# Attention with routed experts on one core: query and key loads moved on the load queue, and the first slots' routing tables counted in another way

## The chip, the cores and the metric

One core of one Trainium2 chip runs the whole program. The metric is device time in microseconds (us) of one execution, lower is better; several executions are timed and their median is given. Beside the timed executions there is one profiled execution, whose trace is quoted here.

The engines are named as the profile names them: PE is TensorE (matmuls and transposes), DVE is VectorE, ACT is ScalarE, POOL is GpSimd, SP is SyncE, which here only issues DMAs. An engine's DMA issues appear under its name with a q (SPq, POOLq).

## The reference: what is computed

Attention over q, k, v of shape (8, 12, 448, 64): each row of q and k is normalised by its root mean square and scaled by a gain, then a softmax over 448 keys, then the product with v. The result, seen as 3584 tokens of 768 columns, goes through a layer of 8 experts, of which each token uses the one with the largest gate logit.

```python
q_n, k_n = rmsnorm(q, g_q), rmsnorm(k, g_k)
attn = softmax(q_n @ k_n.T / sqrt(64))            # per batch and head
x = (attn @ v).transpose(0, 2, 1, 3).reshape(3584, 768)
logits = x @ w_gate + modality_bias[modality_id]  # 8 experts
e_idx = argmax(logits); gate_w = softmax(logits)[e_idx]
out[t] = gate_w[t] * (relu(x[t] @ w1[e]) @ w2[e])   # e = e_idx[t]
```

## The kernel before

**Units and beats.** Attention is cut into 48 units, each of one batch element and two heads. A unit takes seven beats, and beat n of the program is column block j = n mod 7 of unit i = n // 7. The steps of all units are laid out by hand over the beats, from beat -22 to 335; the table `PLAN` and the function `when` (line 1272) say at which beat each step of unit u is issued. Every engine works through its own instructions in the order in which they were issued, and waits on semaphores where it needs another engine's result.

**The steps of a unit.** `load` (line 789) fetches q and k of a unit, or of two units at once, from device memory by a DMA of SP; the buffers `r1` hold six units of each, so the load of unit u overwrites unit u - 6. `sumsq` squares on ACT (tile `xrw` from `r`) and sums on DVE; `rstd` makes the reciprocal root; `norm` multiplies on POOL (`xrw` from `r` and `at_hlw`; it is the last reader of the loaded buffer). `tr` transposes on PE, and ACT and DVE copy the result as a high and a low part into `xw` and `w1w`; 64-partition pieces of these are then moved by DMAs of SP (line 882, `w1w<-xw` and `w2ha<-xw`), eight per unit, four after the key's transpose and four after the query's. `sa` (line 946) multiplies queries by keys for the row maximum, which DVE takes; `mt` (line 957) transposes the seven maxima, and one small DMA of SP (line 962) puts them where `st` needs them. `st` (line 974) are the scores again, transposed and with the maximum inside; ACT takes the exponent; `av` (line 1013) is the product with v; POOL and DVE add the columns for the softmax sums (`csum`).

Relative to unit u (beat 7u is its first `st`), the key's transpose is at beat 7u - 21, the query's at 7u - 18, the first `sa` at 7u - 14, `mt` at 7u - 6, the squares at 7u - 50 (q) and 7u - 49 (k), and the norm at 7u - 26. From unit 10 on, loads come for two units at a time: the key's at beat 7u - 57, the query's at 7u - 54, u even. The first units have beats of their own in `PLAN["first"]`. Before the first beat the queue gets the loads of units 0, 1, then 2 and 3 together, the four gain loads, then 4 and 5 together; 6 and 7 follow together at beat -12, the key's first.

**Small steps in between.** Routing needs many steps on a few elements per partition. They stand in two lists (`fast`, `slow`), and `pump` (line 1191) takes one or two per beat and issues them between the steps of attention; most are DVE instructions (line 53 in the trace, through the wrapper `Deferred`).

**Tables of the first slots.** After the tokens of six of the eight batch elements have been routed, `tables1` (line 1215) makes index tables for the first three slots of the expert layer. A slot is one expert's block of 256 tokens. `blocks` turns the eight counts into whole blocks by a cast, a shift and a cast back, `prefix` adds them up in three rounds of a copy and an add, and `tables` (line 211) makes from this the slot's expert, its first row, its rows of the list and its rows of the weights. For these tables `taken` is None; `tables2` calls the same function for the other slots later, with `taken` given.

**Expert layer.** Fourteen slots follow, each two matrix products in three passes of high and low parts (`ph`, line 565; `py`, line 595), with weights and tokens gathered by DMAs of POOL.

`gate_consts` (line 148), which makes routing constants on POOL, is issued at beat `PLAN["gc"]` = 24. `warm` (line 1221) puts matmuls on nothing into the beats before attention is under way; they feed no result.

Of the kernel before, what the change touches and what calls it, by code (L numbers as in the profile page):

```python
# [66 lines left out]
def kernel(  # L67
# [80 lines left out]
    def gate_consts():  # L148
# [8 lines left out]
        for tf, ti in iotas:  # L157
            GP.tensor_copy(out=tf, in_=ti)
        GP.tensor_scalar(out=ie8, in0=i_e[:, 0:NE], scalar1=float(NE), scalar2=None, op0=ALU.add)
# [15 lines left out]
    i_vt = iota_f("i_vt", [128, 4], [[128, 4]], cm=1)  # L175
    i_tok = cp.tile([CP, B, NCH], I32, name="i_tok")
# [33 lines left out]

    def tables(nm, ns, cnt, nb, taken, e_prev, half_blocks=None):
# [18 lines left out]
        ci = prefix(nb, nm + "_px", nv)  # L230
        dd = tl("dd", [128, nv])
        V.tensor_tensor(out=dd, in0=nb, in1=ci, op=ALU.subtract)
# [24 lines left out]
        def sel(src, n_):  # L257
            r = tl(n_, [128, ns])
            V.tensor_tensor(out=t3, in0=oh, in1=src.unsqueeze(1).to_broadcast(sh), op=ALU.mult)
            V.tensor_reduce(out=r, in_=t3, op=ALU.add, axis=AX.X)  # L260
            return r
# [3 lines left out]
        V.tensor_tensor(out=js, in0=js, in1=isb, op=ALU.add)  # L265
# [4 lines left out]
        V.tensor_scalar(out=eb, in0=es, scalar1=float(NT), scalar2=None, op0=ALU.mult)  # L270
        V.scalar_tensor_tensor(out=js, in0=js, scalar=float(TB), in1=eb, op0=ALU.mult, op1=ALU.add)
        V.tensor_tensor(out=cs, in0=cs, in1=eb, op=ALU.add)
# [8 lines left out]
        V.tensor_scalar(out=eb[:, 0:nn], in0=js[:, 0:nn], scalar1=float(NE * NT - TB), scalar2=0.5,  # L281
# [487 lines left out]
    if True:  # L769
# [365 lines left out]
        def route_pos(b):  # L1135
# [26 lines left out]
            if b == NB1 - 1:  # L1162
                state["runa"] = cp.tile([128, NE], F32, name="runa")
                V.tensor_copy(out=state["runa"], in_=state["run"])
# [50 lines left out]
        def tables1():  # L1215
            nb1 = blocks(state["runa"], "nb1", 0)
# [10 lines left out]
        for u, n in ((0, 1), (1, 1), (2, 2)):  # L1227
            load(u, n)
        load_gains()
        load(4, 2)  # L1230
# [44 lines left out]
        for u in range(NU):  # L1275
# [23 lines left out]
            if u == 6:  # L1299
                put(-12, "load", u, 2, (1, 0))  # L1300
            elif u in (8, 9):
                put(when("ld", u), "load", u)
            elif u > 9 and u % 2 == 0:
                put(when("ld", u) + 1, "load", u, 2, (1,))
                put(when("ld", u) + 4, "load", u, 2, (0,))

        for n in range(P["start"], NJ * NU):
# [86 lines left out]
            if n == P["lz"]:  # L1394
                SY.dma_start(l_d.rearrange("(p r) w -> p (r w)", p=128), zt)
            if n == P["gc"]:
# [222 lines left out]
```

## Time and profile before

| | us |
|---|---|
| Median of 3 timed executions | 1083.87 |
| Lowest and highest of them | 1081.62 and 1086.3 |
| The profiled execution, its own time | 1088.99 |
| Its span, first to last instruction | 1087.2 |
| PE busy in the span | 1047.1 (96%) |
| DVE busy | 782.4 (72%) |
| POOL busy | 704.7 (65%) |
| ACT busy | 696.1 (64%) |
| Mean granted PE clock, of full speed | 0.986 |

Attention lies from the start to about 585 us, the slots of the expert layer from there to 1058 us, and a short end after that. In the trace, a row of the timeline gives the start, the time it lasted, the engine, the line, the operation, the tile written and the tiles read; an "xN" row merges N instructions; brackets give the idle time of that engine before the row and what released it. L52 and L53 are the wrapper's lines, so such rows are told apart by their tiles.

### The profile page before, as it was taken

The page shows a single profiled execution, that of the slowest core. Times are in us where ns is not written, and L with a number is a line of the kernel's source. Part 1 is how long each engine was busy: PE and PEld are TensorE (multiplying, and loading weights), DVE is VectorE, ACT ScalarE, POOL GpSimd, SP SyncE. Part 2 cuts the span into 40 slices and gives each one's busy share as a digit, 9 for nine tenths or more (in the row PEclk, how much of TensorE's full clock was granted, in tenths as well). Part 3 has the DMA queues.
Part 4 walks back from the last instruction along what each step waited for, and adds up shares of the span by engine and source line. Part 5 has one row for each costly group of instructions (what it writes and reads, how often), then busy time and mean ns, then how long its engine had stood idle before and what let it go on. Part 6 is the DMA issues. An engine that isn't in the chain of part 4 may idle for free.

```text
span 1087.2 us, 18988 instructions
## 1 busy us (share of the span) xinstructions
PE 1047.1 (96%) x6536; PEld 808.6 (74%) x6536; DVE 782.4 (72%) x1351; ACT 696.1 (64%) x1293; POOL 704.7 (65%) x728
## 2 busy tenths in 40 slices
PE   8899999989999999999999999999999999999996
PEld 7645555545555555555556999999999999999995
DVE  5676778968779887798878897667655676566740
ACT  6787888868888787786665555555545555455531
POOL 6787777777876878688776566664455544656451
PEclk9899999989999999999999999999999999999998
DMA  7775767757876669673684822533284422244161
GB/s 177 173 179 123 167 161 170 176 122 163 169 163 165 154 168 165 151 166 90 131 263 132 219 61 78 155 119 93 55 289 147 117 85 67 84 117 117 46 219 61
DMA packets 151704, 153.72 MB, mean 141 GB/s; under 512 B 73434, under 2 KB 141486, under 8 KB 151088
## 3 DMA queue, kind: packets, MB, share of 16 engines
q1 hardware_dynamic: 126244, 110.59, 42.7%
q0 software_dynamic: 25328, 41.82, 12.4%
q8 instruction: 54, 0.88, 0.4%
q14 instruction: 50, 0.41, 0.2%
q10 hardware_dynamic: 28, 0.01, 0.0%
HBM read 150.31 MB, written 33.39 MB: 169 GB/s over the span
## 4 chain that ended last, share of the span: by engine, by line
PE 74%; DMA 8%; DVE 6%; issue 5%; POOL 4%; ACT 2%; SPq 0%; POOLq 0%; DVEq 0%; ACTq 0%
PE ph L565 19%; PE py L595 18%; PE av L1013 11%; PE st L974 11%; DMA w1w<-xw 5%; PE sa L946 4%; PE tr L869 3%; PE xt L1070 2%; DVE at_hlw L52 2%; POOL r2w L52 1%; PE sm L1028 1%; POOL xrw L52 1%; PE warm L1223 1%; ACT xw L52 1%; DVE xw L52 1%
## 5 line engine op out<-in xcount | busy, mean ns | idle before, releaser
L565 PE MATMUL ph<-xw,w1w 128*128 128x256 f32 x2016 | 246.6, 283 | 1.4 <-DVE xw L52 0.8
L565 PEld LDWEIGHTS ph<-xw,w1w 128*128 128x128 f32 x2016 | 244.0, 192 | 3.8 <-issue 1.4
L52 DVE TENSOR_REDUCE at_hlw<-sa 128x1 f32<-128x448 f32 x336 | 205.7, 617 | 42.8 <-PE sa L946 24.4
L974 PE MATMUL st<-w1w 128*128 128x448 f32 (+1 forms) x480 | 177.1, 418 | 0.8 <-DMA w1w<-xw 0.6
L946 PE MATMUL sa<-w1w 128*128 128x448 f32 (+1 forms) x288 | 112.2, 390 | 20.0 <-ACT w1w L52 5.8
L52 POOL TENSOR_TENSOR r2w<-r2w 128x448 f32<-128x448 f32 (+1 forms) x72 | 82.1, 1140 | 64.4 <-DVE r2w L52 23.8
L52 ACT ACTIVATE r2w<-st 128x448 f32<-128x448 f32 x168 | 90.7, 543 | 48.5 <-PE st L974 40.6
L974 PEld LDWEIGHTS st<-w1w 128*128 128x128 f32 (+1 forms) x480 | 85.4, 191 | 45.4 <-ACT r2w L52 15.6
L52 POOL DMA_INDIRECT r<-in_moe_w_dram,tb_w x60 | 78.1, 1301 | 57.8 <-DVE w1w L52 42.5
L595 PE MATMUL py<-w2lw,hhw 128*128 128x384 f32 x448 | 113.7, 334 | 0.0
L52 ACT ACTIVATE hhw<-ph 128x512 fp32r<-128x512 f32 x56 | 33.5, 598 | 120.9 <-PE ph L565 102.0
L52 DVE TENSOR_TENSOR w1w<-r,w1w 128x768 fp32r<-128x768 f32 x112 | 103.4, 953 | 8.9 <-ACT w1w L52 7.3
L52 ACT CAST w1w<-xw 64x448 fp32r<-64x448 f32 x188 | 105.5, 561 | 3.4 <-issue 1.4
L52 POOL DMA_INDIRECT r2w<-in_moe_w_dram,tb_vi x48 | 51.0, 1062 | 86.3 <-DVE w2lw L52 73.7
L52 DVE TENSOR_TENSOR w2lw<-r2w,w2ha 128x1536 fp32r<-128x1536 f32 x28 | 49.1, 1757 | 79.2 <-issue 50.3
L52 ACT ACTIVATE at_w2lw<-st 128x448 f32<-128x448 f32 x168 | 90.5, 544 | 22.6 <-PE st L974 17.5
L974 PE MATMUL st<-w1w,w2ha 65*128 65x448 f32 x288 | 101.1, 371 | 1.1 <-DMA w1w<-xw 1.1
L52 POOL TENSOR_TENSOR xrw<-r,at_hlw 112x512 f32<-112x512 f32 x95 | 98.0, 1051 | 5.0 <-PE tr L869 4.5
L52 ACT CAST w1w<-r 128x768 fp32r<-128x768 f32 x112 | 95.0, 901 | 0.0
L946 PEld LDWEIGHTS sa<-w1w 128*128 128x128 f32 (+1 forms) x288 | 55.8, 194 | 35.1 <-issue 10.5
L52 POOL TENSOR_TENSOR r2w<-r2w,at_w2lw 64x448 f32<-64x448 f32 (+1 forms) x48 | 54.7, 1140 | 41.8 <-DVE r2w L52 18.1
L595 PEld LDWEIGHTS py<-w2lw,hhw 128*128 128x128 f32 x448 | 80.9, 188 | 0.0
(313 smaller groups left out, 2208.5 us busy)
## 6 DMA issues: line engine op xcount, KB each, us to landing
w1w<-xw SPq DMA_DIRECT2D x312, 112.0 KB
xg<-xrw SPq DMA_DIRECT2D x14, 768.0 KB
xrw<-xg SPq DMA_DIRECT2D x56, 192.0 KB
r<-in_q_dram SPq DMA_DIRECT2D x22, 448.0 KB
r<-in_k_dram SPq DMA_DIRECT2D x22, 448.0 KB
w2ha<-xw SPq DMA_DIRECT2D x72, 112.0 KB
r2w<-in_v_dram SPq DMA_DIRECT2D x24, 224.0 KB
at_w2lw<-in_v_dram SPq DMA_DIRECT2D x24, 224.0 KB
```

Of the source, the lines that this page charges most:

```text
L52: return fn(*a, **kw)
L565: PE.matmul(ps[:, i], lhsT=lt_, rhs=rt_[:, c], start=n == 0, stop=n == 17)
L595: PE.matmul(ps[n][:, :384], lhsT=lt_[:, j, 128 * t : 128 * t + 128], rhs=rt_[:, 384 * n : 384 * n + 384], start=j == 0 and m == 0, stop=j ...
L869: PE.transpose(sp[:, c], src[:, c], idn[:CP, :CP])
L946: PE.matmul(ps[:, :S], lhsT=t["qq"][r, h, a : a + 128], rhs=t["kk"][h][r], start=True, stop=True)
L974: PE.matmul(ps[:, :S], lhsT=l, rhs=t["qq"][:, h] if first else t["ql"][:, h], start=first and (j != 3 or h == 0), stop=not first and (j != ...
L1013: PE.matmul(t["av"][64 * h : 64 * h + 64, :S], lhsT=vv[r, u % 3, j], rhs=t["p"][r, j], start=c == 0, stop=c == 3)
L1028: PE.matmul(R[g][32 * i : 32 * i + 32, :S], lhsT=sel[:, m], rhs=T[u + i // 2]["cs"][:, i % 2], start=m == 0, stop=False, tile_position=(0, ...
L1070: PE.transpose(ps[:CP, 128 * c : 128 * c + 128], T[u]["xt"][:, c * CP : (c + 1) * CP], idn)
L1223: PE.matmul(wps[:, :128], lhsT=ones, rhs=idn, start=True, stop=True)
```

## The change

Two parts, which share no instruction.

**Loads.** Units 0 to 5 are loaded one by one ahead of the first beat (two loads of 224 KB each, instead of pairs of 448 KB for units 2 and 3, 4 and 5). Units 6 to 9 are loaded one by one at beat 7u - 58 (beat -16 for unit 6, -9 for unit 7; unit 9 keeps its own beat 6). From unit 10 on the pair's query load is at beat 7u - 59, where it was at 7u - 54, and the key load stays at 7u - 57, so the query now comes first.

**Tables of the first slots.** Whole blocks are counted by one comparison of the eight counts with ten thresholds (`thr`, made in `gate_consts`) and a sum; the prefix is a product with a triangle of ones (`upto`, made once on DVE at beat 32) and a sum. This takes the place of `blocks` and `prefix` where `taken` is None. There the copy `runa`, the product for the prefix and nine steps of `tables` go from DVE to POOL, one fused step is split into two, and with `thr` POOL has twelve steps more. DVE has fourteen fewer in the whole program.

```diff
+        GP.tensor_scalar(out=thr, in0=i_s[:, 0 : NT1 // TB], scalar1=float(TB), scalar2=float(TB),
+                         op0=ALU.mult, op1=ALU.add)
...
+    def full_blocks(cnt):
+        sh = [128, NE, NT1 // TB]
+        ge = cp.tile(sh, F32, name="full_ge")
+        V.tensor_tensor(out=ge, in0=cnt.unsqueeze(2).to_broadcast(sh), in1=thr.unsqueeze(1).to_broadcast(sh),
+                         op=ALU.is_ge)
+        nb = cp.tile([128, NE], F32, name="full_nb")
+        V.tensor_reduce(out=nb, in_=ge, op=ALU.add, axis=AX.X)
+        sh = [128, NE, NE]
+        ge = cp.tile(sh, F32, name="full_up")
+        GP.tensor_tensor(out=ge, in0=nb.unsqueeze(1).to_broadcast(sh), in1=upto, op=ALU.mult)
+        ci = cp.tile([128, NE], F32, name="full_ci")
+        V.tensor_reduce(out=ci, in_=ge, op=ALU.add, axis=AX.X)
+        return nb, ci
...
-        ci = prefix(nb, nm + "_px", nv)
+        E = V if taken is not None else GP
+        if taken is None:
+            nb, ci = nb
+        else:
+            ci = prefix(nb, nm + "_px", nv)
...
-        V.tensor_tensor(out=dd, in0=nb, in1=ci, op=ALU.subtract)
+        E.tensor_tensor(out=dd, in0=nb, in1=ci, op=ALU.subtract)
...
-            V.tensor_tensor(out=t3, in0=oh, in1=src.unsqueeze(1).to_broadcast(sh), op=ALU.mult)
+            E.tensor_tensor(out=t3, in0=oh, in1=src.unsqueeze(1).to_broadcast(sh), op=ALU.mult)
...
-        V.tensor_scalar(out=eb, in0=es, scalar1=float(NT), scalar2=None, op0=ALU.mult)
-        V.scalar_tensor_tensor(out=js, in0=js, scalar=float(TB), in1=eb, op0=ALU.mult, op1=ALU.add)
-        V.tensor_tensor(out=cs, in0=cs, in1=eb, op=ALU.add)
+        E.tensor_scalar(out=eb, in0=es, scalar1=float(NT), scalar2=None, op0=ALU.mult)
+        if taken is None:
+            E.tensor_scalar(out=js, in0=js, scalar1=float(TB), scalar2=None, op0=ALU.mult)
+            E.tensor_tensor(out=js, in0=js, in1=eb, op=ALU.add)
+        else:
+            V.scalar_tensor_tensor(out=js, in0=js, scalar=float(TB), in1=eb, op0=ALU.mult, op1=ALU.add)
+        E.tensor_tensor(out=cs, in0=cs, in1=eb, op=ALU.add)
...
-                V.tensor_copy(out=state["runa"], in_=state["run"])
+                GP.tensor_copy(out=state["runa"], in_=state["run"])
...
-            nb1 = blocks(state["runa"], "nb1", 0)
+            nb1 = full_blocks(state["runa"])
...
-        for u, n in ((0, 1), (1, 1), (2, 2)):
-            load(u, n)
+        for u in range(3):
+            load(u)
         load_gains()
-        load(4, 2)
+        for u in range(3, 6):
+            load(u)
...
-            if u == 6:
-                put(-12, "load", u, 2, (1, 0))
-            elif u in (8, 9):
+            if 5 < u < 10:
                 put(when("ld", u), "load", u)
             elif u > 9 and u % 2 == 0:
+                put(when("ld", u) - 1, "load", u, 2, (0,))
                 put(when("ld", u) + 1, "load", u, 2, (1,))
-                put(when("ld", u) + 4, "load", u, 2, (0,))
...
+            if n == P["gc"] + 8:
+                V.tensor_tensor(out=upto, in0=i_e[:, 0:NE].unsqueeze(1).to_broadcast([128, NE, NE]),
+                                in1=i_e[:, 0:NE].unsqueeze(2).to_broadcast([128, NE, NE]), op=ALU.is_le)
```

The same steps of `tables` that the diff shows with `E` also cover the add of `isb` to `js` and the minimum into `eb`.

The order of the instructions on three queues shows what moves. First SP, before the first beats of `sa`, from the loads of units 4 and 5 on (`r_0` is q, `r_1` is k; the last number of a shape is 256, and 112x2 is one unit, 112x4 two). Before:

```order
L794 DMA r_0_150<-in_q_dram 112x4x256
L794 DMA r_1_151<-in_k_dram 112x4x256
L882 DMA w2ha<-xw 64x448 x2
L882 DMA w1w<-xw 64x448 x6
L882 DMA w2ha<-xw 64x448 x2
L882 DMA w1w<-xw 64x448 x2
L794 DMA r_1_151<-in_k_dram 112x4x256
L794 DMA r_0_150<-in_q_dram 112x4x256
L882 DMA w1w<-xw 64x448 x4
L787 DMA r2w<-in_v_dram 128x7x64
```

With the change, from the load of unit 5 on:

```order
L820 DMA r_0_152<-in_q_dram 112x2x256
L820 DMA r_1_153<-in_k_dram 112x2x256
L908 DMA w2ha<-xw 64x448 x2
L908 DMA w1w<-xw 64x448 x6
L820 DMA r_0_152<-in_q_dram 112x2x256
L820 DMA r_1_153<-in_k_dram 112x2x256
L908 DMA w2ha<-xw 64x448 x2
L908 DMA w1w<-xw 64x448 x6
L813 DMA r2w<-in_v_dram 128x7x64
L820 DMA r_0_152<-in_q_dram 112x2x256
L820 DMA r_1_153<-in_k_dram 112x2x256
```

Between the key moves and the query moves of unit 1 there stood the loads of units 6 and 7; now unit 6's stand ahead of all eight moves, and unit 7's come after them.

Second, SP in the steady part, two beats of one pair's loads with the moves around them. Before:

```order
L882 DMA w1w<-xw 64x448 x4
L794 DMA r_1_151<-in_k_dram 112x4x256
L787 DMA at_w2lw<-in_v_dram 128x7x64
L882 DMA w2ha<-xw 64x448 x2
L882 DMA w1w<-xw 64x448 x2
L962 DMA w1w<-xw 1x7x128
L794 DMA r_0_150<-in_q_dram 112x4x256
L882 DMA w1w<-xw 64x448 x4
```

With the change:

```order
L908 DMA w1w<-xw 64x448 x4
L820 DMA r_0_152<-in_q_dram 112x4x256
L820 DMA r_1_153<-in_k_dram 112x4x256
L813 DMA at_w2lw<-in_v_dram 128x7x64
L908 DMA w2ha<-xw 64x448 x2
L908 DMA w1w<-xw 64x448 x2
L988 DMA w1w<-xw 1x7x128
L908 DMA w1w<-xw 64x448 x4
```

The query load went from just ahead of the four query moves of one unit to just behind those of the unit before.

Third, the tables, on DVE. Before, from the copy of the counts on (`at_hlw<-sa` are the row maxima of attention):

```order
L53 COPY runa<-bs_5533 128x8
L52 TENSOR_REDUCE at_hlw<-sa_1_5699 128x1
L53 CAST nb_i<-runa 128x8
L53 TENSOR_SCALAR nb_i<-nb_i 128x8
L53 CAST nb_5718<-nb_i 128x8
L52 TENSOR_REDUCE at_hlw<-sa_2_5745 128x1
L53 COPY ta_px_5719<-nb_5718 128x1
L53 TENSOR_TENSOR ta_px_5719<-nb_5718 128x7
L53 COPY ta_px_5720<-ta_px_5719 128x2
L52 TENSOR_REDUCE at_hlw<-sa_3_5762 128x1
```

With the change, DVE at the same place:

```order
L52 TENSOR_REDUCE at_hlw<-sa_1_5709 128x1
L53 TENSOR_TENSOR full_ge<-runa,thr 128x80
L53 TENSOR_REDUCE full_nb<-full_ge 128x8
L52 TENSOR_REDUCE at_hlw<-sa_2_5754 128x1
L53 TENSOR_REDUCE full_ci<-full_up 128x8
L53 TENSOR_SCALAR ta_tk<-ta_dd 128x8
L52 TENSOR_REDUCE at_hlw<-sa_3_5771 128x1
```

And POOL there, with the change, where before only the 448-column adds, the norms and the DMAs stood:

```order
L53 COPY runa<-bs_5543 128x8
L53 TENSOR_TENSOR full_up<-full_nb,upto 128x64
L53 TENSOR_TENSOR ta_dd<-full_nb,full_ci 128x8
L52 TENSOR_TENSOR xrw<-r_0_152,at_hlw 112x2x4x64
L52 TENSOR_TENSOR xrw<-r_1_153,at_hlw 112x2x4x64
L52 TENSOR_TENSOR r2w<-at_w2lw 128x448
L1196 DMA l_d<-lt_5547,posi_5546 28672x2
L52 TENSOR_TENSOR r2w<-r2w,at_w2lw 64x448
L53 TENSOR_TENSOR ta_t_5733<-ta_oh,ta_dd 128x24
L52 TENSOR_TENSOR at_w2hb<-r2w,at_w2lw 128x448
L53 TENSOR_TENSOR ta_t_5733<-ta_oh,runa 128x24
```

The prefix now goes from DVE to POOL and back twice, and each step of the tables on DVE that reads a POOL result stands between two row maxima. PE's and ACT's instructions are the same, in the same order.

## Rows read from the trace of the kernel before

**Rows 1.** The page, the chain that ended last, shares by engine.

```profile
PE 74%; DMA 8%; DVE 6%; issue 5%; POOL 4%; ACT 2%; SPq 0%; POOLq 0%; DVEq 0%; ACTq 0%
```

**Rows 2.** Windows: PE, PEld, DVE, ACT, POOL busy (count), PE clock, DMA share, GB/s.

```profile
700.00:800.00 100.00, 100.00 (x708) 100.00 (x707) 64.22 (x69) 52.98 (x68) 57.66 (x49) 1.00 0.37 108
```

**Rows 3.** Timeline of ACT and DVE, 10 to 13 us.

```profile
10.86 1.15 ACT L52 ACTIVATE xrw<-r 112x512 f32<-112x512 f32 x2 [2.56 <-DMA r<-in_k_dram]
11.75 0.16 DVE L52 TENSOR_TENSOR gs<-gg 128x1 f32<-128x1 f32 x1 [1.83 <-DMA gg<-in_g_k_dram]
...
12.19 1.27 ACT L52 ACTIVATE w1w<-tr,gs 64x448 fp32r<-64x448 f32 x2 [0.18 <-PE warm L1223]
```

**Rows 4.** Windows of 2 us at the start, columns as in rows 2.

```profile
10.00:12.00 2.00, 2.00 (x21) 1.98 (x18) 0.22 (x2) 1.14 (x2) 0.00 (x0) 1.00 1.11 288
...
30.00:32.00 2.00, 1.94 (x7) 1.89 (x8) 1.01 (x2) 0.00 (x0) 1.92 (x3) 0.50 1.31 191
```

**Rows 5.** Timeline, 23 to 31 us: SP's queue, and PE's first sa of unit 1.

```profile
23.31 0.53 SPq L794 DMA_DIRECT2D r<-in_k_dram  x1
...
23.94 0.48 SPq L794 DMA_DIRECT2D r<-in_q_dram  x1
...
24.52 2.38 SPq L882 DMA_DIRECT2D w1w<-xw  x4
...
30.06 0.71 PE L946 MATMUL sa<-w1w 128*128 128x448 f32 x1 [3.40 <-ACT w1w L52]
```

**Rows 6.** Waits, whole span: us in total, times, longest.

```profile
ACT xrw L52 <- DMA r<-in_q_dram: 13.5, 7, 4.7
```

**Rows 7.** Timeline around two query loads: SP, ACT, PE.

```profile
219.63 0.42 SPq L794 DMA_DIRECT2D r<-in_q_dram  x1
...
227.34 0.63 ACT L52 ACTIVATE xrw<-r 112x512 f32<-112x512 f32 x1 [4.67 <-DMA r<-in_q_dram]
...
227.95 0.71 PE L946 MATMUL sa<-w1w 128*128 128x448 f32 x1 [4.32 <-issue]
...
435.42 0.71 PE L946 MATMUL sa<-w1w 128*128 128x448 f32 x1 [2.30 <-DMA w1w<-xw]
```

**Rows 8.** Timeline of PE, the mt of units 17, 18, 21, 22, 42 and 43.

```profile
215.24 0.28 PE L957 MATMUL mt<-idn,at_hlw 128*7 128x128 f32 x1
...
233.67 0.38 PE L957 MATMUL mt<-idn,at_hlw 128*7 128x128 f32 x1
...
266.72 0.28 PE L957 MATMUL mt<-idn,at_hlw 128*7 128x128 f32 x1
...
277.78 0.28 PE L957 MATMUL mt<-idn,at_hlw 128*7 128x128 f32 x1
...
507.27 0.28 PE L957 MATMUL mt<-idn,at_hlw 128*7 128x128 f32 x1
...
522.64 0.28 PE L957 MATMUL mt<-idn,at_hlw 128*7 128x128 f32 x1
```

**Rows 9.** Windows of line 53 alone: DVE, ACT, POOL busy, PE clock, DMA share, GB/s.

```profile
507.90:528.00 20.10, 12.26 (x28) 0.00 (x0) 0.00 (x0) 0.92 0.55 116
```

**Rows 10.** Timeline of DVE and POOL in the tables, 508 to 527 us.

```profile
508.36 2.04 POOL L52 TENSOR_TENSOR xrw<-r,at_hlw 112x512 f32<-112x512 f32 x2
...
508.87 1.55 DVE L53 CAST nb_i<-runa 128x8 int32<-128x8 f32 x1
...
516.31 0.16 DVE L53 TENSOR_TENSOR ta_dd<-nb,ta_px 128x8 f32<-128x8 f32 x1
...
519.89 1.14 POOL L52 TENSOR_TENSOR r2w<-r2w,at_w2lw 128x448 f32<-128x448 f32 x1 [3.79 <-DVE rs L52]
```

**Rows 11.** Timeline of POOL, a step on 128x8.

```profile
75.10 0.24 POOL L52 TENSOR_SCALAR i_ebase<-i_e 128x8 f32<-128x8 f32 x1
```

**Rows 12.** Timeline of POOL and SP, 205 to 211 us.

```profile
205.24 2.04 POOL L52 TENSOR_TENSOR xrw<-r,at_hlw 112x512 f32<-112x512 f32 x2
...
207.90 2.42 SPq L882 DMA_DIRECT2D w1w<-xw  x4
```

More of the change, by code (lines that the diff above doesn't have):

```diff
@@ L175 @@
     i_vt = iota_f("i_vt", [128, 4], [[128, 4]], cm=1)
+    thr = cp.tile([128, NT1 // TB], F32, name="thr")
+    upto = cp.tile([128, NE, NE], F32, name="upto")
     i_tok = cp.tile([CP, B, NCH], I32, name="i_tok")
@@ L264, in tables @@
         cs = sel(cnt, "cs")
-        V.tensor_tensor(out=js, in0=js, in1=isb, op=ALU.add)
+        E.tensor_tensor(out=js, in0=js, in1=isb, op=ALU.add)
         eb = tl("eb", [128, ns])
@@ L280, in tables @@
         lr = tl("lr", [128, nn], I32)
-        V.tensor_scalar(out=eb[:, 0:nn], in0=js[:, 0:nn], scalar1=float(NE * NT - TB), scalar2=0.5,
+        E.tensor_scalar(out=eb[:, 0:nn], in0=js[:, 0:nn], scalar1=float(NE * NT - TB), scalar2=0.5,
                         op0=ALU.min, op1=ALU.mult)
```

## Prediction

> **What bounds the kernel now.** I read the chain of waits by engine first: PE holds 74% of it, DMA 8%, DVE 6% [rows 1]. Then the windows: in the expert layer PE is busy 100 of 100 us at full clock [rows 2], and the change adds nothing there, so that half can only start earlier. Everything is to be won in attention, wherever PE stands still, and three kinds of places show in the timeline. At the start PE runs on filler matmuls until the first units are ready, so the time there is a chain of latencies: loads, squares, transposes, moves. In the steady part PE is mostly busy, apart from a few holes where ACT waits for a query load; in all ACT waited 13.5 us for query loads, in 7 waits, the longest 4.7 us [rows 6]. And around 508 to 528 us DVE's routing steps hold up the row maxima.
>
> **How one hole works.** The query load of a pair is issued at 219.63 us, ACT reaches the squares of its first unit four beats later and waits 4.67 us, until 227.34; behind this wait stand the exponents that PE's next score blocks need free, so PE is idle for 4.32 us before its next `sa` [rows 7]. This `sa` takes 0.71 us, as the one after the 3.40 us stop at 30.06 us does [rows 5], and in the window after that stop the granted clock is 0.50, the lower level, 1.2 GHz [rows 4]. So a stop of some microseconds costs its length and then some. The unit from one `mt` to the next took 18.43 us there (215.24 to 233.67); the same place in the period of four units takes 11.06 us (266.72 to 277.78) [rows 8]. The hole cost 7.4 us.
>
> **Start, loads one by one.** ACT waits 2.56 us for the key load that carries units 2 and 3 before it turns to unit 0's key, and DVE's gain product, which that needs too, waits 1.83 us for the gains, queued behind the same loads [rows 3]. With units 2 and 3 loaded singly, 448 KB less (0.459 MB) stand ahead of either. At 288 GB/s, the window in which these loads land, that is 1.6 us, at the 191 GB/s of a later window 2.4 us [rows 4]. I take 1.8, nearer the first, which is the place itself; the bounds are 0 (the gains may land by their own latency) and 2.4. All that follows in the start hangs on it, and the PE time it shortens is filler.
>
> Here a rule speaks against the change. The Trainium skill (DMA: Bandwidth & Descriptors, section Bandwidth) wants DMAs batched to 1 MiB or more and shows small ones at lower rates. By that rule halving the transfers would lower the rate and eat this term: 0 in the place of 1.8. No row here tells the sizes apart, since all that is in flight is mixed.
>
> **Start, units 6 and 7.** Both loads of this pair, 0.918 MB, are issued at 23.31 and 23.94 us, directly ahead of the four query moves of unit 1 at 24.52; PE then waits 3.40 us, until 30.06, for the first `sa` that uses moved pieces [rows 5]. At 191 to 288 GB/s these bytes are 3.2 to 4.8 us, the size of the wait. (The row names ACT, whose copy ended before; the moves are what is left.) In the new order unit 6 goes ahead of all eight moves, some 4 us earlier, and unit 7 after them. I leave 0.5 of 3.40 and add 0.8 for the clock: 2.9 + 0.8 = 3.7. Bounds: 0, if unit 6's load just holds the moves as long; 5.5, if all of the wait and about 2 us of half-clock time go.
>
> **Steady loads.** The query load moves from 4 beats ahead of its squares to 9; a beat is 11.06 / 7 = 1.6 us, so it is issued some 8 us earlier, more than the longest wait of 4.7. It no longer stands directly ahead of four query moves: at 435.42 PE's `sa` was released by such moves after 2.30 us [rows 7]. The waits: 13.5 less 1.7 in the start leaves 11.8, of which the hole above is 4.7. Two other long ones belong to the 2.30 us stop and to a shorter one. At the price of the first (7.4 us for 4.67, 1.6 per us) all 11.8 would be 18.7, but the short ones hardly reach PE. I count the first at 7.4, the second at half of it, 3.7, and nothing else, 11.1, and take 10, since some DMA wait stays. Bounds: 13.5, all of ACT's waits at their length, and -4, below.
>
> Is the buffer free so early? The load waits for the norm of the unit it overwrites. Norms of that beat start on POOL at 205.24 and last 2.04, to 207.28; SP then has its four moves from 207.90 to 210.32 [rows 12], and the new load comes after these. So POOL is about 3 us ahead.
>
> **Tables.** In 20.1 us DVE spends 12.26 us on 28 routing steps [rows 9]. An undisturbed one (`ta_dd`) takes 0.16 us [rows 10], so some 4.5 us would do; the rest is waiting inside instructions. The cast `nb_i` starts at 508.87, takes 1.55 us and ends at 510.42, where POOL's norms end (508.36 + 2.04 = 510.40) [rows 10]. The Trainium skill (SBUF, section Who interferes with whom) says that DVE and GpSimd share a port pair, held for a whole instruction. The trace agrees here: 510.42 against 510.40.
>
> Of the 28 steps 18 go; the 10 that stay take about 1.8 us, so DVE gets 10.4 us back and has three new steps, at 0.16 to 1.55 us each. Against it stand six places where DVE now waits for a POOL step (0.24 us each by its kind [rows 11]), in the worst case behind one large add of 1.14 [rows 10]: up to 1.4 us each, 8.4. POOL's twelve steps are 12 x 0.24 = 2.9 us, and POOL itself now waits for DVE twice in the prefix, with two norms queued behind; its cover is an idle time of 3.79 us right after [rows 10]; beyond it the norms come late by the rest, and the transposes that need them are five beats off. What of it reaches the end: unit 43 took 15.37 us (507.27 to 522.64) [rows 8], 4.3 over 11.06. I take 2.5 of these. Bounds: 4.3 and -3, if the round trips cost more than the freed steps. The steps for `upto` and `thr` lie in beats where nobody waits on them: 0.
>
> **Sum.** 1.8 + 3.7 + 10 + 2.5 = 18.0 us. The profiled execution took 1088.99 us (span 1087.2 and 1.8 around it): 1088.99 - 18.0 = 1071.0. That execution is 5.1 us above the median of 1083.87; since holes of this kind come and go, I expect the median to lose less, some 13 us, and to arrive at the same 1071.
>
> **Rivals.**
> - *The loads pile up.* The query load now goes out with the key load and a value load, 448 + 448 + 224 KB, every other time with a store of 672 KB too; 1.15 to 1.84 MB at 191 to 288 GB/s is 4 to 9.6 us, and the next key moves are 4 beats, 6.3 us, away. For it: DMA share 1.31 in one window [rows 4]. Against it: the first `sa` that needs these moves is six beats further. Then the steady part gives 3, the start 3.9, the tables 2.5: 1088.99 - 9.4 = 1079.6.
> - *Tables lose.* The six hand-overs meet POOL's adds and give -3 in the place of 2.5: 1088.99 - 15.5 + 3 = 1076.5.
> - *SP stands still, slower.* The load now comes two beats after the norm that frees its buffer, and SP works in order: if POOL is over 3 us later against SP than in rows 12, SP waits there with the key load, the value load and then the moves behind it, in each of 19 pairs. At 1 us of PE per pair, 19 us, less 8 from start and tables: 1088.99 + 11 = 1100. Against it: the 3 us of lead.
> - *It does not do what it says:* the waits on query loads come from crowded DMA, not from the late issue, and return as waits of moves. That is the first rival by another door, and has its price and chance.
>
> **Chances.** Forecast 0.63, piled loads 0.20, tables 0.12, SP 0.05. A difference of 0.5%, 5.4 us, is about what a measurement of this kernel can tell: faster means under 1078.5. The forecast gives 0.60 faster and 0.03 same; piled loads 0.08, 0.11 and 0.01 slower; tables 0.08 and 0.04; SP 0.05 slower: 0.76, 0.18, 0.06. Range: all terms at their upper bounds would be 1063.3 (25.7 us); above, the piled loads with 1.5 us to spare: 1063 to 1081.
>
> **What would show it.** ACT's squares no longer wait for query loads after the start; the first `sa` of unit 1 follows with no 3.4 us stop, and the windows there keep clock 1.0; no unit lasts 18 us; steps of line 53 in the tables are well under 12 us. Wrong, if PE's stops return with `w1w<-xw` as releaser, if SP's queue waits for POOL's norms at the query loads, or if DVE waits for POOL in the tables.

## The result, and the profile after

The changed kernel takes 1071.67 us, the median of four executions (1071.28 to 1074.59), against 1085.09 for the kernel before, timed beside it (1081.62 to 1087.21, four): a ratio of 0.9885, with a 95% interval of 0.9852 to 0.9918. The forecast was 1071.0, in a range of 1063 to 1081, and "faster by over 0.5%". The execution profiled here took 1071.33, its span 1069.3, 17.9 us less than the span before.

Where the 17.9 us come from is read by setting the two traces side by side at `mt`, which each unit has once. The lead of a kernel is the time of `mt` before less the time of the same `mt` in it. (Line numbers of the changed kernel are some 26 higher: `sa` 972, `mt` 983, load 820, moves 908.)

| lead at `mt` of unit, us | 6 | 8 | 17 | 18 | 19 | 42 | 43 | 45 | 47 |
|---|---|---|---|---|---|---|---|---|---|
| changed kernel | 2.70 | 4.23 | 4.66 | 12.02 | 10.17 | 16.95 | 19.26 | 17.07 | 17.94 |

So the start gave 2.7, units 7 and 8 another 1.5, and the steady part from unit 8 to 42 gave 12.7. Where the tables are made they gave nothing: 2.3 won in unit 43 and 2.2 lost again in 44. A second trace of the same kernel (below) has 2.92, 1.53 and 11.86 for the first three.

**Steady part.** The waits, as in [rows 6]:

```profile
ACT xrw L52 <- DMA r<-in_q_dram: 1.8, 1, 1.8
```

One wait of 1.8 us is left, in the start; there were 7 with 13.5 us. SP's queue, ACT's squares and PE's `mt`, where [rows 7, 8] had the 18.43 us unit:

```profile
203.26 2.44 SPq L908 DMA_DIRECT2D w1w<-xw  x4
205.79 0.54 SPq L820 DMA_DIRECT2D r<-in_q_dram  x1
206.43 0.47 SPq L820 DMA_DIRECT2D r<-in_k_dram  x1
206.95 0.49 SPq L813 DMA_DIRECT2D at_w2lw<-in_v_dram  x1
209.24 2.40 SPq L908 DMA_DIRECT2D w1w<-xw  x4
...
217.92 0.62 ACT L52 ACTIVATE xrw<-r 112x512 f32<-112x512 f32 x1
...
210.58 0.28 PE L983 MATMUL mt<-idn,at_hlw 128*7 128x128 f32 x1
221.65 0.28 PE L983 MATMUL mt<-idn,at_hlw 128*7 128x128 f32 x1
```

The load goes out as soon as SP has issued the moves ahead of it (203.26 + 2.44 = 205.70), ACT's square has no bracket, so it waited for nothing, and the unit takes 11.07 us. Unit 36 went from 15.52 to 11.42, unit 26 from 12.60 to 11.48.

**Start.** SP's queue and PE's first `sa` of units 1 and 2, beside [rows 5], and the windows after (columns as in [rows 2]):

```profile
25.76 0.58 SPq L813 DMA_DIRECT2D r2w<-in_v_dram  x1
26.44 0.59 SPq L820 DMA_DIRECT2D r<-in_q_dram  x1
27.07 0.46 SPq L820 DMA_DIRECT2D r<-in_k_dram  x1
27.63 1.35 SPq L908 DMA_DIRECT2D w2ha<-xw  x2
29.08 3.78 SPq L908 DMA_DIRECT2D w1w<-xw  x6
...
25.61 0.44 PE L972 MATMUL sa<-w1w 128*128 128x448 f32 x1 [0.38 <-DMA w1w<-xw]
...
33.40 0.44 PE L972 MATMUL sa<-w1w 128*128 128x448 f32 x1 [1.86 <-DMA w1w<-xw]
```

```profile
34.00:36.00 2.00, 1.87 (x7) 1.31 (x6) 1.47 (x3) 0.80 (x2) 0.79 (x1) 0.60 0.83 240
36.00:38.00 2.00, 2.00 (x8) 1.77 (x7) 0.62 (x1) 0.58 (x2) 0.47 (x1) 0.54 0.92 207
```

The stop at unit 1 shrank from 3.40 to 0.38 us, but a new one of 1.86 stands before the first `sa` of unit 2, and the granted clock falls to 0.54 behind it. The releaser is a move, and ahead of unit 2's eight moves stand a value load and unit 7's two loads.

**Tables.** DVE and POOL around the place where unit 44 loses what unit 43 won, then PE:

```profile
503.23 1.15 POOL L52 TENSOR_TENSOR r2w<-r2w,at_w2lw 128x448 f32<-128x448 f32 x1
504.45 1.15 POOL L52 TENSOR_TENSOR at_w2hb<-r2w,at_w2lw 128x448 f32<-128x448 f32 x1
...
505.99 0.27 POOL L53 TENSOR_SCALAR ta_eb<-ta_js 128x3 f32<-128x3 f32 x1
506.34 2.04 POOL L52 TENSOR_TENSOR xrw<-r,at_hlw 112x512 f32<-112x512 f32 x2
...
506.29 1.11 DVE L53 TENSOR_SCALAR ta_lr<-ta_eb,i_pt 128x3 int32<-128x3 f32 x1 [1.40 <-POOL ta_eb L53]
...
507.98 0.47 PE L972 MATMUL sa<-w1w 128*128 128x448 f32 x1 [1.76 <-DVE at_hlw L52]
```

`ta_lr` waits 1.40 us for POOL's last table step, which was queued behind two large adds, then takes 1.11 us on three columns, beside POOL's norms; the row maxima wait behind it, and PE for them. DVE's line 53 in the 20.1 us that answer to [rows 9]:

```profile
491.00:511.10 20.10, 9.14 (x19) 0.94 0.52 122
```

9.14 us on 19 steps, where it was 12.26 on 28. They are not the same steps: 13 do the work of the 28 (5.63 us, from 491 to 502), and six that came later before have moved up (3.51 us). Over all the table steps of line 53 it is 11.12 us on 24, where it was 14.36 on 39. Of the 13, ten had been there before, where they took 1.82 us together; now they take 5.01, most of it in this one and in `ta_le` (1.13):

```profile
492.74 1.99 DVE L53 TENSOR_SCALAR ta_tk<-ta_dd 128x8 f32<-128x8 f32 x1 [0.32 <-POOL ta_dd L53]
```

### The profile page after: what moved, and what is told of

The parts are those of the page before. It is cut to its first block, busy times and chain, and to the rows that moved or that the text cites. A ratio compares the mean times of both kernels' runs of the same rounds, so it can differ in the third digit from the quotient of the medians.

```text
span 1069.3 us, 19016 instructions
## 1 busy us (share of the span) xinstructions
PE 1040.7 (97%) x6536; PEld 804.7 (75%) x6536; DVE 779.2 (73%) x1337; ACT 696.2 (65%) x1293; POOL 710.3 (66%) x740
## 4 chain that ended last, share of the span: by engine, by line
PE 82%; DVE 5%; POOL 4%; issue 4%; DMA 3%; ACT 2%; SPq 0%; POOLq 0%; DVEq 0%; ACTq 0%
PE ph L591 21%; PE py L621 20%; PE av L1039 12%; PE st L1000 12%; PE sa L972 5%; PE tr L895 3%; PE xt L1096 2%; PE sm L1054 2%; DVE at_hlw L52 2%; POOL r2w L52 1%; PE warm L1249 1%; PE sm L1061 1%; PE mt L983 1%; DVE xw L52 1%; PE sa L967 1%
## 5 line engine op out<-in xcount | busy, mean ns | idle before, releaser
L52 ACT ACTIVATE yw<-py,ltn 128x384 f32<-128x384 f32 x55 | 29.3, 578 | 77.0 <-PE py L621 48.8
```

The costliest lines, as they stand in the source:

```text
L52: return fn(*a, **kw)
```

## The experiments

Leads are against the profiled execution of the kernel before; the ratios are to executions of that kernel timed together with the other. Its median was 1089.72 beside the first four kernels and 1085.72, 1085.45 and 1083.95 beside the later groups, so times of different groups are compared by their ratios. Kernels with one execution, the profiled one, have no ratio.

### One part at a time

**Steady query loads alone.**

```diff
+                put(when("ld", u) - 1, "load", u, 2, (0,))
                 put(when("ld", u) + 1, "load", u, 2, (1,))
-                put(when("ld", u) + 4, "load", u, 2, (0,))
```

> The kernel before, with only the query loads of the pairs from unit 10 on moved from beat 7u - 54 to 7u - 59; start loads and tables as before. Theory (the late issue of the query load is what makes ACT wait, and these waits alone account for the steady part): the trace of the changed kernel gained 12.7 us between units 8 and 42, so this kernel should take about 12.7 us less than before, some 1072.5; ACT's waits for query loads after 60 us go from about 11.8 us to under 0.5, and units 18 and 36 take about 11.1 to 11.4 us from one mt to the next. Rival (the loads only pile up elsewhere and need the lighter start to pay): under 5 us gained, with PE's stops returning as waits for moves, w1w from xw.

**The start's loads alone** (units 0 to 9).

```diff
...
+        for u in range(3, 6):
+            load(u)
...
+            if 5 < u < 10:
                 put(when("ld", u), "load", u)
...
```

> The kernel before, with only units 0 to 5 loaded singly and units 6 to 9 loaded singly at beat 7u - 58; steady query loads and tables as before. Theory: 4.25 us gained, as the traces stood apart at unit 8, so about 1080.8; the first sa of unit 1 at about 25.6 us instead of 30.06, and a new stop of about 1.9 us at the first sa of unit 2. In steady units 18 and 36 nothing changes: 18.4 and 15.5 us. Rival (the 4.25 us are filler that the later holes take back): under 1.5 us.

**The table part alone** (`full_blocks` and the steps on POOL, in the kernel before).

> The kernel before, with only the table part: full blocks counted by one comparison, a dozen steps on POOL; all loads as before. Theory (from the traces: unit 43 gains 2.3 us, unit 44 gives 2.2 back, because DVE waits 1.4 us for POOL's last table step and is then locked 1.1 us behind POOL's norms): within 1 us of before, 1084 to 1086. Rival (what the prediction said): 2.5 us less, 1082.5, with DVE's line 53 between 488 and 510 us at half its busy time and no stop of PE behind it. A third: slower by 3 us if the hand-overs meet POOL's adds.

**Both load parts with the old tables.**

> The changed kernel with the old tables: both load parts, no table part. Theory (start 4.25 plus steady 12.7, tables nothing): 17 us less than before, 1068 by the profiled execution's scale and within 1 us of the changed kernel's 1071.67 by the medians. Rival (tables are worth the predicted 2.5): about 1074.

| kernel | median (lowest to highest, executions) | ratio to before, 95% | lead at 6 | 8 | 17 | 18 | 19 | 42 | 45 | 47 |
|---|---|---|---|---|---|---|---|---|---|---|
| steady alone | 1077.20 (1074.68 to 1078.32, 6) | 0.9893 [0.9857, 0.9929] | -0.11 | 0.52 | 0.93 | 8.29 | 6.37 | 13.07 | 13.45 | 13.40 |
| start alone | 1082.82 (1077.36 to 1090.02, 12) | 0.9942 [0.9912, 0.9972] | 2.93 | 2.66 | 2.73 | 2.73 | 2.51 | 6.25 | 6.65 | 6.70 |
| tables alone | 1086.25 (1080.91 to 1095.45, 12) | 0.9980 [0.9949, 1.0011] | -0.32 | 0.62 | 0.12 | 0.02 | -0.05 | 0.62 | 0.81 | 0.76 |
| both loads | 1071.24 (1069.37 to 1074.16, 6) | 0.9848 [0.9812, 0.9885] | 3.59 | 4.24 | 4.67 | 12.02 | 10.10 | 17.59 | 17.86 | 18.00 |

The steady loads win 12.6 us from unit 8 to 42 by themselves, and their ratio says 11.7 (1.07% of 1089.72): the theory held, the piled loads did not come. The start alone leads by 2.5 to 2.9 us up to unit 19, less than the 4.25 expected, since the 1.5 us of units 7 and 8 are not in it; its ratio says 6.3 (3.1 to 9.6), more than that lead, and whether the lighter start also makes later holes rarer is not shown. The interval of the tables' ratio contains 1, but the predicted 2.5 us as well; that they give nothing is read from units 43 and 44 (27.77 us together before, 27.59 here) and from both loads without them, which stand where the changed kernel stands.

The 1.5 us of units 7 and 8 can be told apart in these traces. Unit 7 takes 15.92 to 15.96 us in four of the five traces with the old tables (17.47 in the fifth, units 0 to 5 singly, below) and 15.06 to 15.08 in all nine with the new. All five have a stop of PE of 1.05 us that is only 0.19 with the tables alone and 0.17 in the changed kernel; in the kernel before it is this one:

```profile
95.13 0.60 PE L869 MATMUL tr<-idn,xrw 112*128 112x112 f32 x4 [1.05 <-POOL xrw L52]
```

The only instructions of the table part that come so early are `thr` and `upto`, so they change when POOL's norm comes; by which way was not taken apart. Unit 6 pays 0.2 us for it. Unit 8 takes 8.51 to 8.86 us in the four traces with late query loads and 7.91 to 7.93 in the ten with early ones: the stop of 0.3 to 0.65 us for a move is gone there. One figure was not expected: with the start alone, unit 36 lost its hole (11.58 us) and unit 30 got one (15.08 against 11.08). While the query loads are late, the holes move from trace to trace: with the start alone the lead falls to -0.39 us at unit 30 and is 6.25 at unit 42. The two kernels of the four that keep late loads spread over 13 and 15 us in twelve executions, the two others over 4 and 5 in six.

### The start, taken apart

**Only units 0 to 5 singly, units 6 and 7 as before.**

```diff
-        for u, n in ((0, 1), (1, 1), (2, 2)):
-            load(u, n)
+        for u in range(3):
+            load(u)
         load_gains()
-        load(4, 2)
+        for u in range(3, 6):
+            load(u)
```

> The kernel before, with only units 0 to 5 loaded singly; units 6 and 7 together at beat -12 as before. It splits the start. Theory (two independent gains, as the prediction has them): mt of unit 0 comes 1.4 to 2.2 us earlier, and the stop before the first sa of unit 1 stays at about 3.4 us, so unit 1's mt is also about 1.8 us earlier and not 4. Rival (the stop at unit 1 belongs to the crowded first loads, not to the pair 6 and 7): the stop shrinks below 1 us here too, and unit 1's mt is about 4 us earlier.

One execution, 1087.67 us. PE's first `sa` of unit 1, and ACT in the steady part:

```profile
28.03 0.49 PE L946 MATMUL sa<-w1w 128*128 128x448 f32 x1 [4.24 <-DMA w1w<-xw]
...
226.50 0.63 ACT L52 ACTIVATE xrw<-r 112x512 f32<-112x512 f32 x1 [4.37 <-DMA r<-in_q_dram]
...
367.23 0.63 ACT L52 ACTIVATE xrw<-r 112x512 f32<-112x512 f32 x1 [4.40 <-DMA r<-in_q_dram]
```

`mt` of unit 0 comes 2.87 us earlier (1.4 to 2.2 were expected), unit 2's 2.25, and the stop at unit 1 is still there, 4.24 us: two independent gains, and the releaser of that stop is now named as the moves. The whole is no faster, because a second large hole opened at unit 30 (17.95 us, lead from 1.13 to -5.74) behind ACT's wait of 4.40. What the start wins can be lost while the query loads are late.

**Unit 7's loads behind the moves of unit 2.**

```diff
-                put(when("ld", u), "load", u)
+                put(0 if u == 7 else when("ld", u), "load", u)
```

> The changed kernel with one edit: unit 7's loads at beat 0, behind the moves of unit 2, in the place of beat -9, ahead of them. Theory (the new stop of 1.86 us before the first sa of unit 2 comes from unit 7's two loads being issued ahead of unit 2's moves, 1.2 us of SP and their transfer): the stop falls under 0.8 us, the granted clock in 34 to 38 us rises from about 0.57 to over 0.9, and the lead at unit 2's mt grows from 2.85 to between 4 and 5.5 us, 1.2 to 2.6 us less in all, about 1069.5. Rival (SP's issue of the eight moves alone, 4.5 us, makes the stop): under 0.5 us.

1070.87 us (1068.70 to 1072.05, four), ratio 0.9867 [0.9844, 0.9890]: not to be told from the changed kernel. The stop at unit 2 is gone, but there is one of 1.59 us for a later move, behind the loads of units 8 and 7 together:

```profile
40.03 0.45 PE L1000 MATMUL st<-w1w,w2ha 65*128 65x448 f32 x1 [1.59 <-DMA w1w<-xw]
```

The low clock was not gone either: it came at 18 to 26 us, with no stop of PE over 0.7 us before it. A trace with the change's own start and the low clock in the same place (the last table steps on DVE, below) has no stop at unit 2 either. So this run leaves open whether the order on SP or the clock sets the start; the next two kernels, timed together, ask that.

**Unit 7's loads at beat 4**, and **the changed kernel again**, unedited, timed together with it.

```diff
-                put(when("ld", u), "load", u)
+                put(4 if u == 7 else when("ld", u), "load", u)
```

> The changed kernel with unit 7's loads at beat 4, behind the moves of unit 2 and behind unit 8's loads and a value load, to be set against the changed kernel in the same call. Theory (with unit 7's loads at beat 0 the stop at unit 2 went but a 1.59 us stop of st for a move came at 40.03, since two loads more stood ahead of the next moves): neither stop, mt of unit 8 at 111.3 to 112 us, and 1 to 2 us less than the changed kernel by the medians. Rival (the start's time is set by when the granted clock falls, which differed between executions of one and the same start: once at 34 to 38 us, once at 18 to 26): within 0.5 us of the changed kernel by the medians, with a low-clock stretch of about 4 us somewhere before 40 us again.

> The changed kernel, unedited, for a second trace of its start and as the measure for the other kernel of this call. Theory (order on SP sets the stop at unit 2): again a stop of 1.5 to 2.5 us before the first sa of unit 2 and the low clock at 34 to 38 us. Rival (where the clock falls is chance): the stop is under 0.8 us or over 3 us, and mt of unit 2 is over 1 us from 44.75. Ratio to before between 0.985 and 0.992.

| kernel | median (lowest to highest, executions) | ratio to before, 95% | lead at 2 | 6 | 8 | 42 | 47 |
|---|---|---|---|---|---|---|---|
| unit 7 at beat 4 | 1067.45 (1066.56 to 1068.30, 5) | 0.9829 [0.9802, 0.9856] | 5.81 | 5.65 | 7.20 | 20.41 | 21.39 |
| changed kernel again | 1071.50 (1068.90 to 1073.27, 6) | 0.9868 [0.9842, 0.9894] | 3.10 | 2.92 | 4.45 | 16.31 | 16.73 |

The executions of the two do not overlap, and the medians differ by 4.05 us, more than the 1 to 2 expected (`mt` of unit 8 came at 110.10): this version beats both the kernel before and the changed one. SP's queue of unit 7 at beat 4, and its windows after unit 2 began:

```profile
25.60 0.62 SPq L813 DMA_DIRECT2D r2w<-in_v_dram  x1
26.32 1.24 SPq L908 DMA_DIRECT2D w2ha<-xw  x2
27.65 3.81 SPq L908 DMA_DIRECT2D w1w<-xw  x6
31.56 0.54 SPq L820 DMA_DIRECT2D r<-in_q_dram  x1
32.14 0.48 SPq L820 DMA_DIRECT2D r<-in_k_dram  x1
32.66 0.46 SPq L813 DMA_DIRECT2D r2w<-in_v_dram  x1
33.22 2.44 SPq L908 DMA_DIRECT2D w1w<-xw  x4
```

```profile
34.00:36.00 2.00, 2.00 (x13) 1.76 (x12) 1.23 (x2) 1.12 (x3) 1.54 (x2) 1.00 1.12 272
36.00:38.00 2.00, 1.85 (x13) 1.44 (x11) 0.62 (x1) 1.98 (x5) 1.92 (x3) 1.00 1.05 237
```

Unit 2's moves go out 1.3 us earlier, no stop of PE from 14 to 48 us is longer than 0.66, and the clock is 1.00 there. The changed kernel again had a stop at unit 2 (1.62 us) and 0.50 from 34 to 38 us, as the theory wanted. In the eight traces that have the change's own start, though, the lead at unit 6 runs from 0.83 to 4.47 us, 2.7 in the mean: one of them (the last table steps on DVE, below) had no stop at unit 2 and the low clock at 18 to 26. So the order on SP moves the median, and where the clock falls adds scatter to it; what makes it fall at 18 us in some executions is not shown.

### How much lead the query load needs

```diff
-                put(when("ld", u) - 1, "load", u, 2, (0,))
                 put(when("ld", u) + 1, "load", u, 2, (1,))
+                put(when("ld", u) + 2, "load", u, 2, (0,))
```

> The changed kernel, with the pair's query load at beat 7u - 56 in the place of 7u - 59: behind the key load, 2 beats earlier than before instead of 5. It asks how much lead the loads need. Theory (the lead alone matters, ACT's wait of 4.7 us in unit 18 is 3 beats of 1.6 us): unit 18 keeps a wait of ACT of some 1.5 us and takes 11.1 to 12.5 us instead of 11.07 (18.43 before); all in all 0 to 3 us more than the changed kernel between units 8 and 42. Rival (what counts is that the query load leaves the place directly ahead of the query's moves): the same time as the changed kernel within 0.5 us. Second rival (the two loads of a pair must not go together): unit 18 over 14 us.

1071.56 us, one execution. From unit 8 to 42 it wins 12.6 us, unit 18 takes 11.05 us, and no square after the start waits for a query load: "lead alone" fell, the first rival held. SP of the kernel before (the second row is the last of the four moves in the first), then of this one, and its square:

```profile
213.88 4.83 SPq L882 DMA_DIRECT2D w1w<-xw  x4
215.70 3.02 SPq L882 DMA_DIRECT2D w1w<-xw  x1
218.81 0.78 SPq L962 DMA_DIRECT2D w1w<-xw  x1
219.63 0.42 SPq L794 DMA_DIRECT2D r<-in_q_dram  x1
```

```profile
207.03 0.54 SPq L820 DMA_DIRECT2D r<-in_k_dram  x1
207.62 0.51 SPq L813 DMA_DIRECT2D at_w2lw<-in_v_dram  x1
208.19 0.55 SPq L820 DMA_DIRECT2D r<-in_q_dram  x1
210.46 2.42 SPq L908 DMA_DIRECT2D w1w<-xw  x4
...
219.16 0.62 ACT L52 ACTIVATE xrw<-r 112x512 f32<-112x512 f32 x1
```

Two beats earlier in the program, 3.2 us, is 8.0 us earlier on SP: from 4.39 us after unit 17's `mt` (215.24) to 3.65 before it (211.84). The three beats more of the changed kernel add 1.1. What counted was that the load passes the key's moves and the small `mt` move. SP starts these moves at the same distance from unit 17's `mt` in both kernels (1.4 us before it), but takes 4.83 us over them instead of 2.42, and the load stood behind them. The difference is the issue of the last move, for which the trace shows no wait: it takes 2.94 to 3.34 us in all four traces with late query loads and 0.59 or 0.60 in the other ten. What holds it up is not shown.

### The tables, taken apart

**Counting by comparison, every step on DVE.**

```diff
-        E = V if taken is not None else GP
+        E = V
```

(The product `full_up` and the copy `runa` go to DVE too.)

> The changed kernel with the new way of counting, but every table step on DVE. It parts the counting from the move to POOL. Units 43 and 44 took 27.8 us together before, 27.65 in the changed kernel and 27.5 with the old tables and the new loads. Theory (the hand-overs to POOL eat what the counting frees): 25.5 to 26.7 us here, and PE's wait for DVE between 485 and 515 us falls below 2 us in all. Rival (what costs is DVE locked behind POOL's norms, in whichever steps fall there): 27 us or more, again with single small steps of over 1 us.

**The last six steps back on DVE.**

```diff
-        E.tensor_tensor(out=js, in0=js, in1=isb, op=ALU.add)
+        V.tensor_tensor(out=js, in0=js, in1=isb, op=ALU.add)
...
-        E.tensor_scalar(out=eb[:, 0:nn]
+        V.tensor_scalar(out=eb[:, 0:nn]
```

> The changed kernel with the last six table steps (js, eb, cs and the rows of the list) back on DVE; counting, the prefix product, dd and the two products of sel stay on POOL. Theory (the 1.40 us wait of ta_lr for POOL's last step, behind two adds, makes the 1.76 us stop of PE in unit 44): that stop is gone, and units 43 and 44 together take 25.5 to 26.5 us instead of 27.65. Rival: the steps back on DVE meet POOL's norms and are locked, 27 us or more.

**The table steps thinned out**, one in even and three in odd beats in the place of three in each.

```diff
...
-                    if state["n"] - last[0] < gap[kind] or (
+                    if state["n"] - last[0] < (gap[kind] if kind != "tab" else state["n"] % 2 == 0) or (
...
```

> The changed kernel, with the table steps of the first slots put out at four in two beats instead of six. DVE is busy 3.9 of 4 us in most windows from 488 to 516 us, whichever version of the tables runs, and units 43 and 44 took 27.4 to 27.8 us in four of five. Theory (it is the density of DVE steps, each now and then locked behind POOL's norms, and not their number, that holds up the row maxima): spaced, units 43 to 45 lose 2 us or more of the 5 that they stand above the same units four earlier (10.87 + 11.66 us for units 27 and 28, 22.5), about 1069.5 us. Rival (each hand-over and each lock costs where it falls, spaced or not): within 1 us of the changed kernel.

| us from `mt` of unit 42 to that of | 43 | 44 | 45 | sum |
|---|---|---|---|---|
| kernel before | 15.37 | 12.40 | 9.98 | 37.75 |
| old tables, new loads | 14.93 | 12.56 | 9.99 | 37.48 |
| changed kernel | 13.06 | 14.59 | 9.98 | 37.63 |
| counting on DVE | 14.89 | 12.55 | 9.96 | 37.40 |
| last six steps on DVE | 13.09 | 18.42 | 9.98 | 41.49 |
| thinned out | 12.76 | 12.57 | 11.85 | 37.18 |

Counting on DVE was executed once (1072.50 us), and so were the last six steps on DVE (1071.27). Five of six sums agree within 0.6 us: neither the counting nor the move to POOL shows a gain here (from `mt` of unit 42 to that of unit 47 the changed kernel takes 58.68 us and 59.25 in its second trace, the old tables with the new loads 59.26). The thinned version (1070.46 us, 1068.43 to 1075.14, four; ratio 0.9858 [0.9793, 0.9922]) missed the 2 us expected: it wins 0.45, and to unit 47 it takes 59.3 us, as the others do. Counting on DVE shows why. Its new steps, and POOL's work beside two of them:

```profile
493.25 1.62 DVE L53 TENSOR_TENSOR full_ge<-runa,thr 128x80 f32<-128x80 f32 x1
494.91 0.24 DVE L53 TENSOR_REDUCE full_nb<-full_ge 128x8 f32<-128x80 f32 x1
496.40 0.20 DVE L53 TENSOR_REDUCE full_ci<-full_up 128x8 f32<-128x64 f32 x1
496.64 1.54 DVE L53 TENSOR_TENSOR ta_dd<-full_nb,full_ci 128x8 f32<-128x8 f32 x1
```

```profile
492.73 2.05 POOL L52 TENSOR_TENSOR xrw<-r,at_hlw 112x512 f32<-112x512 f32 x2
497.00 1.14 POOL L52 TENSOR_TENSOR r2w<-r2w,at_w2lw 64x448 f32<-64x448 f32 x1
```

`ta_dd`, 0.16 us in [rows 10], now takes 1.54 and ends at 498.18, where POOL's add ends (498.14); `full_ge` ends at 494.87, POOL's norms at 494.78. Both have two inputs, while the reduces between them take 0.20 and 0.24. The Trainium skill (SBUF — State Buffer, section Who interferes with whom) says that DVE steps with two inputs there contend with GpSimd's reads and that reduces never do; these rows agree. So the rival held: which step is held up changes, how long DVE is held up hardly does. Line 53 takes 14.36 us over the whole table before, 14.35 with the old tables and the new loads and 13.79 with the counting on DVE; in the changed kernel 11.12, beside which DVE waits 2.65 us for POOL's table steps (0.32, 0.35, 0.58 and 1.40). With the last six steps on DVE the 1.40 us wait was gone, but the units took longer, the opposite of the theory:

```profile
505.14 0.74 PE L963 MATMUL sa<-xw 128*128 128x448 f32 x1 [1.92 <-DVE at_hlw L52]
508.68 0.74 PE L968 MATMUL sa<-w1w 128*128 128x448 f32 x1 [1.28 <-DVE at_hlw L52]
```

```profile
504.00:508.00 4.00, 2.26 (x7) 1.52 (x7) 3.96 (x6) 1.08 (x2) 3.75 (x4) 0.50 0.27 61
508.00:512.00 4.00, 3.32 (x13) 0.79 (x13) 3.49 (x14) 1.42 (x4) 2.08 (x2) 0.50 0.28 61
```

Two stops close together, 3.2 us in all, and the clock at its lower level for 8 us: unit 44 took 18.42 us.

## Why the prediction came out right

The time was right to 0.7 us of the median, and the main mechanism is shown. That the sum came out so close is luck: two of its four terms were too large by 5 us together, and what it left out made up for them (2.7 more in the steady part, 1.5 in units 7 and 8, 0.9 in units 46 and 47; in the second trace 1.9, 1.5 and 0.3).

- **Start, loads one by one: 1.8.** With them alone the lead is 2.87 us at unit 0, over the upper bound of 2.4, and 2.25 at unit 2. At unit 0 the eleven traces that have units 0 to 5 singly lead by 0.43 to 2.87, 1.7 in the mean: the size was right. The reading was kinder than its row: ACT's wait of 2.56 us lies mostly in the window from 8 to 10 us, which moved 200 GB/s and not 288; by that the estimate would have been 2.3. The rule that the prediction cites from the Trainium skill (DMA: Bandwidth & Descriptors, section Bandwidth), by which smaller transfers would have made it 0, did not show here: from 2 to 10 us 232 GB/s were moved before and 248 with these loads alone. (The section's table is of DMAs that GpSimd issued; these are SP's.)
- **Start, units 6 and 7: 3.7.** This term failed. The stop at unit 1 went as said (3.40 to 0.38), but the step "unit 7 after them" looked only at unit 1's moves: unit 7's loads now stood ahead of unit 2's, which the same trace shows 1.86 us late, and the clock fell there instead. Both start terms together gave 2.7 us at unit 6 (mean of eight traces 2.7), not 5.5. With unit 7 at beat 4 the lead is 5.65 in its one trace, what the two terms promised, so it is the place that was wrong and not the sizes. The 0.8 us "for the clock" in the term had no working, and no run parts it from the stop. What was late next should have been asked of unit 2 as well. Two of the prediction's own signs show it: a stop of PE with `w1w<-xw` as releaser, and a granted clock of 0.60 and 0.54 where 1.0 was expected.
- **Units 7 and 8** were not in the sum: 1.5 us. Unit 7's 0.85 comes with the table part, whose `thr` and `upto` had been put at 0 because nobody waits in their beats; unit 8's 0.68 comes with the steady query loads.
- **Steady loads: 10.** 12.7 were measured, 12.6 alone. The mechanism is right, the term too small (over the ten traces with early query loads it is 11.9 to 13.4). The lower bound of -4 follows from none of the rivals. Of the holes, unit 18 gave 7.36 (7.4 was said), unit 36 4.10 (3.7 was said), units 26 and 38 another 1.12 and 0.96, which had been counted at nothing; 1.85 came back in unit 19, also not foreseen. There a routing step, `oh`, runs beside POOL's norms and takes 2.69 us in the changed kernel; with the hole of unit 18 still in place it takes 0.18. PE's two waits for DVE in unit 19 are 0.43 and 0.39 us; that `oh` makes the rest of the 1.85 is not shown:

```profile
224.46 2.69 DVE L53 TENSOR_TENSOR oh<-i_e,ei 112x32 f32<-112x32 f32 x1
```

- That the load is issued "some 8 us earlier" by five beats was right by the clock (9.2 us, from 4.39 after unit 17's `mt` to 4.79 before it) and wrong in its reason: two beats did 8.0 of them, by passing the late moves.
- **Tables: 2.5.** They gave 0.1 in units 43 and 44, within the bounds. The step that failed is "DVE gets 10.4 us back": the held-up time was taken to belong to the steps that went, and it belongs to POOL's large instructions. The ten steps that stay, put at 1.8 us, took 5.01; over the whole table line 53 got 3.2 us back (14.36 to 11.12), and waits of 2.65 us for POOL's steps, a sign that the prediction had named, took most of that again. Even the rival was not it: no loss of 3.
- **The rivals.** Piled loads: excluded by the steady loads alone. SP standing still at the load: in 17 of the 19 pairs it did not, the load follows the move ahead of it by 0.09 to 0.11 us. At 75.33 us it stood 2.10 for POOL's norm, and at 118.86 for 0.47, and no unit shows a loss for it. That the early issue does nothing: excluded, ACT's waits are gone.

That the median would lose less than the single trace, some 13 us against 18, came out so (13.4 and 17.7); the reason given, holes that come and go, is what the start alone shows in units 30 and 36. How much less depends on the executions too: beside other kernels the median of the kernel before was up to 1089.72.

## What to carry to other kernels

Where one queue issues everything, look for a load's place among the transfers that wait for engines, and not only for its lead in the program's count: here two beats that passed such a group were worth 8.0 us. Then look at what stands behind the load, for the next group and the one after. Small steps that last long beside another engine's large instructions were not made much cheaper here by having fewer of them; the time must be read from that other engine. And in a single execution a gain at the start can vanish in a later hole: read such a gain with the late loads mended, or from many executions.

## What had not been expected of the hardware

ACT's wait for a query load and what it costs the unit (against 11.06 us in units 18 and 30, 11.48 in unit 26, 11.42 in unit 36) go together, across kernels:

| ACT's wait, us | 0.31 | 1.30 | 1.89 | 2.37 | 2.38 | 3.01 | 4.40 | 4.67 |
|---|---|---|---|---|---|---|---|---|
| unit longer by | 0.16 | 1.03 | 1.12 | 4.02 | 3.65 | 4.10 | 6.89 | 7.37 |
| kernel, unit | start, 36 | tables, 30 | before, 26 | start, 30 | tables, 36 | before, 36 | first six, 30 | before, 18 |

Waits up to 1.9 us cost less than their length; from 2.4 us on a unit pays 1.4 to 1.7 times the wait. ("Start" and "tables" are those parts alone, "first six" is units 0 to 5 singly.)

Unit 2's eight moves keep SP busy for 5.2 us in the changed kernel (27.63 to 32.86), and unit 7's two loads ahead of them for 1.1 (26.44 to 27.53); with these two gone the moves went out 1.3 us sooner, the stop of PE and the low clock behind it went too, and the median fell by 4.05. The Trainium skill (DMA: Bandwidth & Descriptors, section Issuing engines are not separate DMA queues) calls the sequencer's time to start a DMA usually small beside the DMA itself. In this start it was not small beside the bytes: a move of 112 KB takes SP 0.6 us to issue, and at the 201 to 289 GB/s of the windows from 28 to 34 us its bytes take an estimated 0.4 to 0.6. How long such a move takes until it has landed is not in the trace.

The stretch from unit 47's `mt` to the end of the span lasted between 518.1 and 523.1 us in the traces, whatever the change, so a difference of a few microseconds between spans tells nothing about attention; leads do.
